# RWKV-5 attention into a top-1 mixture of experts on one Trainium2 core: a new order of turns, sends, logits and weight pieces

## The chip, the cores and the metric

The kernel runs on one core of a Trainium2 chip. The core's engines each run their own instruction stream and meet only at semaphores: TensorE (PE for its matmuls, PEld for its weight loads), VectorE (DVE), ScalarE (ACT), GpSimd (POOL) and SyncE (SP), which here only starts DMA transfers. Matmuls write PSUM, which TensorE, VectorE and ScalarE reach; all else lies in SBUF or in HBM. The metric is the device time of one execution in microseconds (us), as the median of several runs. Lower is better.

## The reference

The attention keeps a 48 x 48 state for each of 4 x 8 (batch, head) pairs over 768 steps; its output is read as 3072 tokens of 384 numbers, and each token goes through one of 8 experts.

```python
for t in range(S):                                   # S = 768
    cur = np.einsum('bhd,bhe->bhde', u[None] * kt, vt)
    y[:, :, t] = np.einsum('bhd,bhde->bhe', rt, state + cur)
    state = w[None, :, :, None] * state + np.einsum('bhd,bhe->bhde', kt, vt)
...
logits = x @ w_gate                                  # x: 3072 x 384
expert_idx = np.argmax(logits, axis=1)
probs = np.exp(logits - logits.max(-1, keepdims=True))
probs /= probs.sum(-1, keepdims=True) + 1e-09
gate_w = probs[np.arange(N), expert_idx]
for e in range(E):                                   # E = 8
    mask = expert_idx == e
    ye = np.maximum(x[mask] @ w1[e], 0.0) @ w2[e]    # 384 -> 1024 -> 384
    out[mask] = gate_w[mask, None] * ye
```

## The kernel before

All of the profiled time is the function `straight`; a second function, `general`, serves inputs that do not fit its assumptions (a decay out of bounds, more than 416 tokens for one expert) and does not run here.

**Attention.** The work is cut into 16 units, unit i = 4 b + hp: batch b, head pair hp. The 768 steps of a unit are 6 chunks of 128. Within a chunk the recurrence is done in closed form: r and k are scaled by powers of the decay (`scale`, L220, VectorE, with the tables `TT`, L114 to 124), the scores of a chunk are one 128 x 128 matmul for each head (`p_scores`, L247), kept only below the diagonal (`mask`, L261, VectorE), with r*u*k on the diagonal. That diagonal comes from `pairs` (L226, the product r*k into `rp`), `p_own` (L235, TensorE sums it with u), `own_t` (L244, VectorE transposes it) and `diag` (L256, twelve pieces on ScalarE that write the identity times the diagonal into `A`; `mask` then puts the scores into the lower part). Between chunks the state is carried: `keys` (L230, GpSimd, k by the decay table `T3`), `p_ds` (L271), `scan` (L279, VectorE). `p_out` (L285, TensorE) multiplies scores and states into `yps`, `out_t` (L304, ScalarE) copies it out. Two units later `p_tr` (L312) turns the result with a selection matrix whose 8 last columns are the gate's weights, so that each token's 96 numbers of this head pair come with 8 partial logits: 104 columns. Chunks 0 to 3 go to the PSUM tile `tr`, chunks 4 and 5 to the same two banks, `X23`, in which `p_scores` puts its chunks 4 and 5 (columns 0 to 255 of a bank; `p_tr` uses 256 to 359). `keep` (L317) copies both into the batch's row buffer `xb` and adds the partial logits up.

**Routing**, once for each batch, from 6 units after its first on: `choose` (L330, argmax and exponentials), `p_rank` (L343) and `slots` (L352) give every token a row in its expert's region of a buffer `rows` in HBM, `gates` (L358) writes the gate into column 96 of every row, `total` (L364) keeps the running counts, and `send` (L369, GpSimd) starts one indirect DMA for each chunk of 128 tokens that scatters their rows. `ids` (L377, GpSimd) writes the token numbers into column 97. It does so ahead of all other writes of its batch, at the end of units 0, 4, 8 and 12. There are two buffers `xb`, so that at units 8 and 12 the buffer must first have been left by the sends of the batch two earlier.

**Experts.** `Pass` (L392) handles up to 416 rows of one expert: `load` (four DMAs), `xT` (VectorE transposes), `L1` (into four PSUM banks, relu on ScalarE), `L2`, and `put` (gate times result, and indirect DMAs by GpSimd that scatter to the output). The first expert is two passes of 256 and 160 rows, so that it can start before the last batch is sent; the last expert's rows from 160 on go through `tokens_out` (L436), 384 wide. Weights are loaded whole (`weights`, L386) into three buffers, two of them there from the start.

**Order.** Each engine works strictly in the order in which the program issues its instructions, and that order is written by hand in the loop over i (L485 to L540). The tile framework adds a wait wherever an instruction touches a tile, or a PSUM bank, that another engine still uses. For unit i the loop issues: `p_own(i)`, `own_t(i)`, `p_scores` of chunks 0 to 3; for a batch that is due, `p_rank` and `slots`; `scale`, `pairs` and `keys` of unit i + 1; `diag(i)`; `p_tr(i-2)`; `p_ds(i)`; `p_scores` of chunks 4 and 5; two masks; `keep(i-2)`; the third mask; `scan(i)`; gates, total and two or three sends; `p_out(i-1)`, `out_t(i-1)`; `choose`, `ids`; the loads of unit i + 3. Loads and weights stand in one queue behind SP, sends behind GpSimd. The tables for all four head pairs are built before the loop: sixteen small VectorE instructions for `TT`, one product `T3c`, four transposes and one copy for `T3`.

Of the kernel before, what the change touches and what calls it, by code (L numbers as in the profile page):

```python
# [29 lines left out]
Q = 2 * D + 2  # L30
CAP = 416
PAD = 320
EARLY = 256
# [7 lines left out]
def straight(tc, rk, vk, w, w1, w2, out, flag):  # L41
# [42 lines left out]
    def load(i):  # L84
        if i >= U:
            return
        b, hp = divmod(i, HP)
        nc.sync.dma_start(rks[i % 3][0:KP], rk[b, hp].rearrange("h p u s -> (h p) u s")[0:KP])
        nc.sync.dma_start(vks[i % 4], vk[b, hp])
# [3 lines left out]
    for i in range(3):  # L93
        load(i)
# [9 lines left out]

# [9 lines left out]
    TT = cp.tile([KP, HP, 2, C], FP32, name="TT")  # L114
    inv = cp.tile([KP, HP], FP32, name="inv")
    nc.vector.reciprocal(inv, pw[:, 6, :])
    nc.vector.tensor_copy(TT[:, :, 0, 0], inv)
    nc.vector.tensor_copy(TT[:, :, 1, C - 1], inv)
    for l in range(7):
        n = 1 << l  # L120
        wn = bc(pw[:, l, :, None], [KP, HP, n])
        nc.vector.tensor_tensor(TT[:, :, 0, n:2 * n], TT[:, :, 0, 0:n], wn, op=ALU.mult)
        nc.vector.tensor_tensor(TT[:, :, 1, C - 2 * n:C - n], TT[:, :, 1, C - n:C], wn, op=ALU.mult)  # L123

    T3c = cp.tile([KP, HP, C], FP32, name="T3c")
    nc.vector.tensor_tensor(T3c, TT[:, :, 1, :], bc(pw[:, 7, :, None], [KP, HP, C]), op=ALU.mult)
    T3 = cp.tile([128, HP, 2 * D], FP32, name="T3")

    def key_decay():
        for hp in range(HP):  # L130
            nc.tensor.transpose(tr[:, hp * 128:hp * 128 + KP], T3c[:, hp, :], ident[0:KP, 0:KP])
        nc.scalar.copy(T3.rearrange("p a (h d) -> p a h d", h=2),
                       tr.rearrange("p (a h d) -> p a h d", a=HP, h=2)[:, :, :, 0:D])
# [13 lines left out]
    def state_decay():  # L147
        nc.gpsimd.memset(dec, 0.0)
        nc.gpsimd.tensor_copy(dec[:, :, :, 1:], bc(pw[:, 7, :, None, None], [KP, HP, D, G - 2]))

# [30 lines left out]
    w1s = [cp.tile([128, DT, F], FP32, name=f"w1s{i}") for i in range(2)]  # L181
    w2s = [cp.tile([128, FT, DM], FP32, name=f"w2s{i}") for i in range(2)]
# [19 lines left out]
    lgs = [ca.tile([128, G, E], FP32, name=f"lg{i}") for i in range(2)]  # L202
    sub, ex, eq = [ca.tile([128, G, E], FP32, name=n) for n in ("sub", "ex", "eq")]
# [10 lines left out]
    def prep(i):  # L214
        if i < U:
            scale(i)
            pairs(i)
            keys(i)

# [6 lines left out]
    def pairs(i):  # L226
        x = rks[i % 3]
        nc.gpsimd.tensor_tensor(rps[i % 2][0:KP], x[0:KP, 0], x[0:KP, 1], op=ALU.mult)  # L228

    def keys(i):  # L230
        hp, v = i % HP, vks[i % 4]
        nc.gpsimd.tensor_tensor(Kds[i % 2], v[:, G:2 * G - 1, :], bc(T3[:, hp, None, :], [128, G - 1, 2 * D]),  # L232
                                op=ALU.mult)
# [74 lines left out]
    W_ = 2 * D + E  # L308
# [8 lines left out]
    def keep(i):  # L317
        b, hp = divmod(i, HP)
        nc.vector.tensor_copy(xbs[b % 2][:, 0:4, hp, 0:2 * D], trv[0][:, :, 0:2 * D])
        nc.scalar.copy(xbs[b % 2][:, 4:G, hp, 0:2 * D], trv[1][:, :, 0:2 * D])  # L320
        for cs, t in ((slice(0, 4), trv[0]), (slice(4, G), trv[1])):
            lg, l = lgs[b % 2][:, cs], t[:, :, 2 * D:]
            if hp == 0:
                nc.vector.tensor_copy(lg, l)
            else:
                nc.vector.tensor_tensor(lg, l, lg, op=ALU.add)
# [3 lines left out]
    def choose(b):  # L330
        lg, oh = lgs[b % 2], ohs[b % 2]
# [8 lines left out]

    rp = tr[:, 4 * W_:4 * W_ + G * E].rearrange("p (c e) -> p c e", e=E)

# [38 lines left out]
    def count(dst):  # L381
        nc.tensor.matmul(tr[:, 480:480 + E], lhsT=ones, rhs=osum, start=True, stop=True, skip_group_check=True)
# [102 lines left out]
    for i in range(U + 1):  # L485
# [16 lines left out]
        if not last:  # L502
            diag(i)
# [612 lines left out]
```

## Time and profile before

| | us |
|---|---|
| median of 14 runs | 432.23 |
| lowest, highest | 427.46, 435.14 |
| the profiled execution | 428.85 |
| its span in the trace | 427.1 |
| PE busy in the span | 391.5 (92%) |
| PEld, DVE, ACT, POOL busy | 263.5, 147.3, 112.3, 189.9 |
| first matmul of the experts (L417) starts | 145.64 |
| mean granted TensorE clock | 0.969 |

The trace records one execution. A line of a view names a source line (L253), an engine and an operation with its tiles, output first. "Busy" is the time in which an engine executes; matmuls are pipelined, and their weight loads (PEld) run beside them. The granted clock is the share of full speed that TensorE was given. The page's rows over time divide the span into 40 slices and give each engine's busy share in tenths. The chain of waits goes back from the last instruction: at each step to what released it. Each group of instructions by line shows the mean duration of one. As context for the steps of the loop, these are the groups of some of its lines (how many instructions, and the mean of one):

| line | engine, what | count | mean ns |
|---|---|---|---|
| L222 | DVE, `scale`, 112 x 1536 | 16 | 2057 |
| L228 | POOL, `pairs`, 112 x 768 | 16 | 2133 |
| L253 | PE, `p_scores`, 128 columns | 384 | 328 |
| L259 | ACT, `diag`, 128 x 128 | 192 | 388 |
| L371 | POOL, one send | 24 | 1249 |
| L417 | PE, `L1` (three widths together) | 432 | 475 |
| L467 | POOL, one `put` transfer | 96 | 983 |

### The profile page before, as it was taken

The page shows a single profiled execution, that of the slowest core. Times are in us where ns is not written, and L with a number is a line of the kernel's source. Part 1 is how long each engine was busy: PE and PEld are TensorE (multiplying, and loading weights), DVE is VectorE, ACT ScalarE, POOL GpSimd, SP SyncE. Part 2 cuts the span into 40 slices and gives each one's busy share as a digit, 9 for nine tenths or more (in the row PEclk, how much of TensorE's full clock was granted, in tenths as well). Part 3 has the DMA queues.
Part 4 walks back from the last instruction along what each step waited for, and adds up shares of the span by engine and source line. Part 5 has one row for each costly group of instructions (what it writes and reads, how often), then busy time and mean ns, then how long its engine had stood idle before and what let it go on. Part 6 is the DMA issues. An engine that isn't in the chain of part 4 may idle for free.

```text
span 427.1 us, 6777 instructions
## 1 busy us (share of the span) xinstructions
PE 391.5 (92%) x2659; PEld 263.5 (62%) x2659; DVE 147.3 (34%) x324; ACT 112.3 (26%) x318; POOL 189.9 (44%) x189
## 2 busy tenths in 40 slices
PE   1799999799769699999999999999999999999993
PEld 0588788588558588858555555555555555455661
DVE  6888887568645221211101201301211211212020
ACT  1567576547534220320200210110120120001100
POOL 4998529539355022250400650560470370276641
PEclk9999999869958999999999999999999999999998
DMA  8956887938902614940900830650560480011101
GB/s 214 274 159 193 241 244 227 317 109 289 374 5 91 210 38 129 344 82 3 345 28 2 254 151 0 188 221 0 135 276 5 80 328 8 11 38 33 32 22 44
DMA packets 26761, 61.36 MB, mean 144 GB/s; under 512 B 17143, under 2 KB 18179, under 8 KB 24672
## 3 DMA queue, kind: packets, MB, share of 16 engines
q1 hardware_dynamic: 21984, 51.29, 38.6%
q0 software_dynamic: 4736, 9.55, 6.4%
q8 instruction: 23, 0.38, 0.4%
q14 instruction: 18, 0.15, 0.1%
HBM read 50.08 MB, written 11.13 MB: 143 GB/s over the span
## 4 chain that ended last, share of the span: by engine, by line
PE 77%; POOL 6%; DMA 5%; DVE 5%; ACT 3%; issue 3%; SPq 0%; POOLq 0%; ACTq 0%; DVEq 0%
PE X L417 32%; PE yps L428 19%; PE dsb L428 10%; DMA rows<-xb,slot 4%; PE X L253 4%; ACT A L259 3%; PE yps L296 3%; PE tr L314 2%; POOL rp L228 2%; POOL rows L371 2%; PE dsb L276 2%; PE dsb L241 2%; PE yps L447 1%; PE dsb L447 1%; PE yps L301 1%
## 5 line engine op out<-in xcount | busy, mean ns | idle before, releaser
L467 POOL DMA_INDIRECT out_dram<-yo,ix x96 | 94.3, 983 | 158.2 <-DVE yo L464 112.2
L417 PE MATMUL X<-xT,w1s 128*128 128x416 f32 (+2 forms) x432 | 136.2, 475 | 3.3 <-DVE xT L409 2.1
L417 PEld LDWEIGHTS X<-xT,w1s 128*128 128x128 f32 x432 | 79.1, 190 | 58.0 <-issue 52.8
L419 ACT ACTIVATE hT<-X 128x416 f32<-128x416 f32 (+2 forms) x72 | 34.5, 479 | 221.7 <-PE X L417 208.5
L428 PE MATMUL yps<-hT,w2s 128*128 128x416 f32 (+2 forms) x288 | 85.8, 451 | 0.7 <-DVE yq L430 0.7
L428 PEld LDWEIGHTS yps<-hT,w2s 128*128 128x128 f32 x288 | 51.4, 190 | 33.4 <-issue 31.2
L259 ACT ACTIVATE A<-ident,own 128x128 f32<-128x128 f32 x192 | 57.9, 388 | 16.1 <-DVE own L245 15.4
L430 DVE STREAM_TRANSPOSE yq<-yps 128x416 f32<-128x416 f32 (+2 forms) x18 | 9.7, 537 | 126.8 <-PE yps L428 126.8
L371 POOL DMA_INDIRECT rows<-xb,slot x24 | 30.0, 1249 | 46.4 <-DVE osum L367 31.8
L428 PE MATMUL dsb<-hT,w2s 128*128 128x416 f32 (+2 forms) x144 | 42.8, 450 | 0.0
L228 POOL TENSOR_TENSOR rp<-rk 112x768 f32<-112x768 f32 x16 | 34.1, 2133 | 9.4 <-DVE TT L123 4.9
L253 PE MATMUL X<-RK 48*128 48x128 f32 x384 | 35.7, 328 | 1.6 <-DVE RK L222 1.6
L428 PEld LDWEIGHTS dsb<-hT,w2s 128*128 128x128 f32 x144 | 25.7, 190 | 15.7 <-issue 15.3
L253 PEld LDWEIGHTS X<-RK 48*128 48x128 f32 x384 | 28.8, 221 | 8.8 <-issue 5.9
L222 DVE TENSOR_TENSOR RK<-rk,TT 112x1536 f32<-112x1536 f32 x16 | 32.8, 2057 | 0.0
L409 DVE STREAM_TRANSPOSE xT<-xs 128x416 f32<-128x416 f32 (+2 forms) x27 | 13.1, 535 | 50.9 <-DMA xs<-rows 50.9
L241 PE MATMUL dsb<-rp,wug 112*2 112x192 f32 x128 | 9.4, 369 | 20.3 <-POOL rp L228 18.1
L296 PE MATMUL yps<-A,vk 128*48 128x128 f32 x384 | 27.0, 296 | 0.0
L296 PEld LDWEIGHTS yps<-A,vk 128*48 128x48 f32 x384 | 22.8, 134 | 2.3 <-issue 0.4
L265 DVE COPY_PREDICATED A<-strict,X 128x512 f32<-128x512 int32 x32 | 22.7, 729 | 4.1 <-ACT A L259 4.1
L232 POOL TENSOR_TENSOR Kd<-vk,T 128x480 f32<-128x480 f32 x16 | 21.7, 1358 | 2.0 <-PE dsb L276 1.3
L306 ACT COPY yT<-yps 112x384 f32<-112x384 f32 x32 | 13.8, 482 | 32.6 <-PE yps L301 32.6
(104 smaller groups left out, 231.2 us busy)
## 6 DMA issues: line engine op xcount, KB each, us to landing
w1s<-in_w_dram SPq DMA_DIRECT2D x8, 1536.0 KB, 8.3
w2s<-in_w_dram SPq DMA_DIRECT2D x8, 1536.0 KB, 11.5
rk<-in_rk_dram SPq DMA_DIRECT2D x16, 672.0 KB, 6.3
vk<-in_vk_dram SPq DMA_DIRECT2D x16, 528.0 KB, 4.3
xs<-rows SPq DMA_DIRECT2D x28, 159.2 KB, 3.9
out_dram<-yo,ix POOLq DMA_INDIRECT x96, 3.8
rows<-zt SPq DMA_DIRECT2D x1, 1176.0 KB, 8.6
xs<-rows SPq DMA_DIRECT2D x4, 98.0 KB, 2.5
```

Of the source, the lines that this page charges most:

```text
L222: nc.vector.tensor_tensor(RKs[i % 3][0:KP].rearrange("p u (c t) -> p u c t", t=C), x[0:KP].rearrange("p u (c t) -> p u c t", t=C), bc(TT[: ...
L228: nc.gpsimd.tensor_tensor(rps[i % 2][0:KP], x[0:KP, 0], x[0:KP, 1], op=ALU.mult)
L232: nc.gpsimd.tensor_tensor(Kds[i % 2], v[:, G:2 * G - 1, :], bc(T3[:, hp, None, :], [128, G - 1, 2 * D]), op=ALU.mult)
L253: nc.tensor.matmul(o, lhsT=r[q, 1, c * C:(c + 1) * C], rhs=r[q, 0, c * C:(c + 1) * C], start=True, stop=True, skip_group_check=True)
L259: nc.scalar.activation(A[:, place(c, h), :], ident, func=ACT.Copy, scale=own[i % 2][:, c, h:h + 1])
L265: nc.vector.copy_predicated(A[:, 4 * k:4 * k + 4, :], bc(m[:, None, :], [128, 4, C]), X01[k])
L296: nc.tensor.matmul(o(c, h), lhsT=v[:, c, h * D:(h + 1) * D], rhs=A[:, place(c, h), :], start=c < 2, stop=c == 0, skip_group_check=True)
L371: s_ = nc.gpsimd.indirect_dma_start(out=rows[:, :], out_offset=bass.IndirectOffsetOnAxis(ap=slot[b % 2][:, c:c + 1], axis=0), in_=xbs[b % ...
L417: nc.tensor.matmul(p[:, 0:self.n], lhsT=w1s[self.e % 3][:, m, f * 128:(f + 1) * 128], rhs=self.t[:, m, 0:self.n], start=m == 0, stop=m == ...
L419: nc.scalar.activation(h[:, f, 0:self.n], p[:, 0:self.n], func=ACT.Relu)
L428: nc.tensor.matmul(p[:, 0:n], lhsT=w2s[self.e % 3][:, f, m * 128:(m + 1) * 128], rhs=self.h[:, f, 0:n], start=f == 0, stop=f == FT - 1, sk ...
L467: s_ = nc.gpsimd.indirect_dma_start(out=out4[:, :], out_offset=bass.IndirectOffsetOnAxis(ap=ix[:, k:k + 1], axis=0), in_=yo[:, k, :], in_o ...
```

## The change

What it does, in the order of the code:

- The loads of r, k and of v, k by chunk are split (`load_rk` at the head of a unit, `load_vk` at its end).
- `p_fill(n)` issues n matmuls of the identity that nobody reads: 14 at the start, 4 in each of units 1 and 2.
- The decay tables are built for one head pair at a time (`decays`, `key_decay`, `p_key_decay`), with both halves of `TT` in one instruction: pair 0 ahead of the loop, pair i + 1 in units 0, 1 and 2. `pairs(0)` and four of the `keys` go to VectorE.
- `turn`: GpSimd copies one element of `own(i)`, so that its work on unit i + 1 starts behind `own_t(i)`.
- A row has 104 columns (`Q`), not 98: the partial logits stay in it, and columns 96 and 97 (gate, number) lie over the first two of them. `keep` is two ScalarE copies of full width, and `choose` sums the four partial logits in one instruction for each batch.
- In the loop, the masks and `p_ds` move ahead of `p_rank`, and `p_tr(i-2)` and `keep(i-2)` ahead of `p_scores` of chunks 4 and 5.
- The results of `p_rank` and `count` lie in the bank `dsb`, no longer in `tr`.
- `ids(b)` comes directly behind `gates(b)` and `total(b)` of its own batch; the sends follow a table, one or two for each of the next units (batch 2: two, then four).
- Weights lie in pieces (`w1` in four, `w2` in three column blocks of 128), in two buffers, each piece refilled as soon as its last use is behind; at the end experts 0 and following are loaded once more without use (`e % E`). `tokens_out` therefore multiplies in 3 x 128 columns.

```diff
-Q = 2 * D + 2
+Q = 2 * D + E
...
-    def load(i):
-        if i >= U:
-            return
-        b, hp = divmod(i, HP)
-        nc.sync.dma_start(rks[i % 3][0:KP], rk[b, hp].rearrange("h p u s -> (h p) u s")[0:KP])
-        nc.sync.dma_start(vks[i % 4], vk[b, hp])
+    def load_rk(i):
+        if i < U:
+            b, hp = divmod(i, HP)
+            nc.sync.dma_start(rks[i % 3][0:KP], rk[b, hp].rearrange("h p u s -> (h p) u s")[0:KP])
+    def load_vk(i):
+        if i < U:
+            b, hp = divmod(i, HP)
+            nc.sync.dma_start(vks[i % 4], vk[b, hp])
...
+    def p_fill(n):
+        for _ in range(n):
+            nc.tensor.matmul(tr[:, 384:512], lhsT=ident, rhs=ident, start=True, stop=True, skip_group_check=True)
...
+    p_fill(14)
...
-    nc.vector.tensor_copy(TT[:, :, 0, 0], inv)
-    nc.vector.tensor_copy(TT[:, :, 1, C - 1], inv)
-    for l in range(7):
-        n = 1 << l
-        wn = bc(pw[:, l, :, None], [KP, HP, n])
-        nc.vector.tensor_tensor(TT[:, :, 0, n:2 * n], TT[:, :, 0, 0:n], wn, op=ALU.mult)
-        nc.vector.tensor_tensor(TT[:, :, 1, C - 2 * n:C - n], TT[:, :, 1, C - n:C], wn, op=ALU.mult)
...
+    def two(h0, nh, first, second, n):
+        a = TTf[:, h0 * 2 * C + first:h0 * 2 * C + first + n]
+        return bass.AP(a.tensor, a.offset, [list(a.ap[0]), [2 * C, nh], [second - first, 2], [1, n]])
+    def decays(h0, nh):
+        nc.vector.tensor_copy(two(h0, nh, 0, 2 * C - 1, 1), bc(inv[:, h0:h0 + nh, None, None], [KP, nh, 2, 1]))
+        for l in range(7):
+            n = 1 << l
+            nc.vector.tensor_tensor(two(h0, nh, n, 2 * C - 2 * n, n), two(h0, nh, 0, 2 * C - n, n),
+                                    bc(pw[:, l, h0:h0 + nh, None, None], [KP, nh, 2, n]), op=ALU.mult)
+    def key_decay(h0, nh):
+        nc.vector.tensor_tensor(T3c[:, h0:h0 + nh, :], TT[:, h0:h0 + nh, 1, :],
+                                bc(pw[:, 7, h0:h0 + nh, None], [KP, nh, C]), op=ALU.mult)
+    def p_key_decay(h0, nh):
+        for hp in range(h0, h0 + nh):
             nc.tensor.transpose(tr[:, hp * 128:hp * 128 + KP], T3c[:, hp, :], ident[0:KP, 0:KP])
-        nc.scalar.copy(T3.rearrange("p a (h d) -> p a h d", h=2),
-                       tr.rearrange("p (a h d) -> p a h d", a=HP, h=2)[:, :, :, 0:D])
+        nc.scalar.copy(T3[:, h0:h0 + nh].rearrange("p a (h d) -> p a h d", h=2),
+                       tr[:, h0 * 128:(h0 + nh) * 128].rearrange("p (a h d) -> p a h d", a=nh, h=2)[:, :, :, 0:D])
...
+    turn = cp.tile([1, 1], FP32, name="turn")
...
-    w1s = [cp.tile([128, DT, F], FP32, name=f"w1s{i}") for i in range(2)]
-    w2s = [cp.tile([128, FT, DM], FP32, name=f"w2s{i}") for i in range(2)]
+    w1s = [[cp.tile([128, DT, FQ], FP32, name=f"w1s{i}{q}") for q in range(4)] for i in range(2)]
+    w2s = [[cp.tile([128, FT, 128], FP32, name=f"w2s{i}{m}") for m in range(DT)] for i in range(2)]
...
+    def pairs(i, eng=None):
         x = rks[i % 3]
-        nc.gpsimd.tensor_tensor(rps[i % 2][0:KP], x[0:KP, 0], x[0:KP, 1], op=ALU.mult)
-    def keys(i):
+        (eng or nc.gpsimd).tensor_tensor(rps[i % 2][0:KP], x[0:KP, 0], x[0:KP, 1], op=ALU.mult)
+    def keys(i, eng=None):
         hp, v = i % HP, vks[i % 4]
-        nc.gpsimd.tensor_tensor(Kds[i % 2], v[:, G:2 * G - 1, :], bc(T3[:, hp, None, :], [128, G - 1, 2 * D]),
-                                op=ALU.mult)
+        (eng or nc.gpsimd).tensor_tensor(Kds[i % 2], v[:, G:2 * G - 1, :], bc(T3[:, hp, None, :], [128, G - 1, 2 * D]),
+                                         op=ALU.mult)
...
     def keep(i):
         b, hp = divmod(i, HP)
-        nc.vector.tensor_copy(xbs[b % 2][:, 0:4, hp, 0:2 * D], trv[0][:, :, 0:2 * D])
-        nc.scalar.copy(xbs[b % 2][:, 4:G, hp, 0:2 * D], trv[1][:, :, 0:2 * D])
-        for cs, t in ((slice(0, 4), trv[0]), (slice(4, G), trv[1])):
-            lg, l = lgs[b % 2][:, cs], t[:, :, 2 * D:]
-            if hp == 0:
-                nc.vector.tensor_copy(lg, l)
-            else:
-                nc.vector.tensor_tensor(lg, l, lg, op=ALU.add)
+        nc.scalar.copy(xbs[b % 2][:, 0:4, hp, :], trv[0])
+        nc.scalar.copy(xbs[b % 2][:, 4:G, hp, :], trv[1])
...
+        nc.vector.tensor_reduce(lg, xbs[b % 2][:, :, :, 2 * D:].rearrange("p c a e -> p c e a"), axis=AX, op=ALU.add)
...
-    rp = tr[:, 4 * W_:4 * W_ + G * E].rearrange("p (c e) -> p c e", e=E)
+    rp = dsb[:, 432:432 + G * E].rearrange("p (c e) -> p c e", e=E)
...
-    def weights(e, which=None):
-        if which in (None, 0):
-            nc.sync.dma_start(w1s[e % 3], w1[e])
-        if which in (None, 1):
-            nc.sync.dma_start(w2s[e % 3], w2[e])
+        nc.tensor.matmul(dsb[:, 480:480 + E], lhsT=ones, rhs=osum, start=True, stop=True, skip_group_check=True)
+        nc.vector.tensor_tensor(dst, dsb[:, 480:480 + E], basef, op=ALU.subtract)
+    def weights1(e):
+        for q in range(4):
+            nc.sync.dma_start(w1s[e % 2][q], w1[e % E, q])
+    def weights2(e, ms=range(DT)):
+        for m in ms:
+            nc.sync.dma_start(w2s[e % 2][m], w2[e % E, m])
...
+                p, y = ybank[t], yt[t].rearrange("p (a m i) -> p m a i", a=HP, m=DT)
+                for m in range(DT):
+                    o = p[:, m * 128:(m + 1) * 128]
+                    for f in range(FT):
+                        nc.tensor.matmul(o, lhsT=self.h[:, f, LAST + t * 128:LAST + (t + 1) * 128],
+                                         rhs=w2s[self.e % 2][m][:, f, :], start=f == 0, stop=f == FT - 1,
+                                         skip_group_check=True)
...
+    sends = {}
+    for b in range(B - 1):
+        for k, cs in enumerate(((0,), (1, 2), (3, 4), (5,)) if b < B - 2 else ((0, 1), (2, 3, 4, 5))):
+            sends[4 * b + 6 + k] = (b, cs)
+    decays(0, 1)
+    scale(0)
+    pairs(0, nc.vector)
+    key_decay(0, 1)
     state_decay()
+    p_scores(0, range(2))
     p_own(0)
     own_t(0)
-    scale(0)
-    key_decay()
+    p_key_decay(0, 1)
     keys(0)
     for i in range(U + 1):
         last = i == U
         b, k = divmod(i - 6, 4)
-        rt = i >= 6
+        rt = i >= 6 and k == 0 and b < B - 1
+        load_rk(i + 3)
         if not last:
             if i > 0:
                 p_own(i)
                 own_t(i)
-            p_scores(i, range(4))
-        if rt and k == 0:
-            p_rank(b)
-            slots(b)
-        prep(i + 1)
+            nc.gpsimd.tensor_copy(turn, own[i % 2][0:1, 0, 0:1])
+            p_scores(i, range(4) if i > 0 else range(2, 4))
+            if 0 < i < 3:
+                p_fill(4)
+        if i + 1 < U:
+            if i + 1 < HP:
+                decays(i + 1, 1)
+            scale(i + 1)
+            if i + 1 < HP:
+                key_decay(i + 1, 1)
+                p_key_decay(i + 1, 1)
+            pairs(i + 1)
+            keys(i + 1, nc.vector if i in (7, 8, 11, 12) else None)
         if i == 0:
             selection()
         if i == 2:
             numbers()
         if not last:
             diag(i)
+            mask(i, 0)
+            mask(i, 1)
+            p_ds(i)
+        if rt:
+            p_rank(b)
+            slots(b)
+        if not last:
+            scan(i)
         if 2 <= i:
             p_tr(i - 2)
-        if not last:
-            p_ds(i)
-            p_scores(i, range(4, G))
-            mask(i, 0)
-            mask(i, 1)
-        if 2 <= i:
             keep(i - 2)
         if not last:
+            p_scores(i, range(4, G))
             mask(i, 2)
-            scan(i)
-        if rt and k < 3:
-            if k == 0:
-                gates(b)
-                total(b)
-            m = 3 if b == B - 2 else 2
-            send(b, range(m * k, min(m * k + m, G)))
+        if rt:
+            gates(b)
+            total(b)
+            ids(b)
+        if i in sends:
+            send(*sends[i])
         if 1 <= i:
             p_out(i - 1)
             out_t(i - 1)
         if i % 4 == 1 and i > 4:
             choose((i - 5) // 4)
-        if i % 4 == 0 and i < U:
-            ids(i // 4)
-        load(i + 3)
-        if i == 4:
+        load_vk(i + 3)
+        if i == 3:
             clear()
-        if i in (9, 11):
-            weights(0, (i - 9) // 2)
+        if i in (12, 13):
+            (weights1, weights2)[i - 12](0)
         if i == 14:
-            weights(1, 0)
+            weights1(1)
+        if i == U - 1:
             count(cnt3)
             nc.vector.tensor_scalar(out=viol[:, 12:13], in0=cnt3[:, 0:1], scalar1=float(EARLY), scalar2=None, op0=ALU.is_lt)
-        if i == U - 1:
+            weights2(1, range(2))
             first.load()
-            weights(1, 1)
+            weights2(1, range(2, DT))
...
     total(B - 1)
+    ids(B - 1)
     send(B - 1, range(G))
...
-    weights(2)
...
+    for k in range(2, n):
+        p, o = passes[k], passes[k - 1]
+        if k < n - 1:
+            p.L1()
+            passes[k + 1].xT()
+            weights1(p.e + 2)
+            o.L2()
+            o.put()
+            if o.e + 2 <= E:
+                weights2(o.e + 2)
+        else:
+            o.L2()
+            p.L1()
+            weights1(p.e + 2)
+            o.put()
         if k + 2 < n:
             passes[k + 2].load()
-        if passes[k].e + 2 < E:
-            weights(passes[k].e + 2)
-    passes[-2].L2()
-    passes[-1].L1()
-    passes[-2].put()
-    passes[-1].L2(n=LAST)
-    passes[-1].put(LAST)
-    passes[-1].tokens_out()
+    p.L2(n=LAST)
+    p.put(LAST)
+    p.tokens_out()
```

## The prediction

> **What bounds the kernel now.** I read four views: the page's rows over time, the stretches, the chain of waits, the timeline. A digit of the page is a fortieth of the 427.1 us span, 10.7 us.
>
> ```profile
> PE   1799999799769699999999999999999999999993
> PEclk9999999869958999999999999999999999999998
> ```
>
> From the 14th slice on TensorE is full: there the mixture of experts runs at TensorE's own pace, and nothing but TensorE's work or a late tile can move it. The losses are in the first 13 slices, in the loop over 16 units. Three stretches of that loop (stretch, length, then busy us of PE, PEld, DVE, ACT, POOL, then granted clock, DMA share, GB/s):
>
> ```profile
> 67.10:73.70 6.60, 6.60 (x114) 5.52 (x116) 5.30 (x9) 4.68 (x15) 6.00 (x5) 1.00 0.75 249
> 73.70:83.30 9.60, 6.59 (x110) 5.46 (x108) 6.20 (x14) 5.68 (x18) 5.03 (x5) 0.99 0.88 277
> 83.30:94.90 11.60, 11.16 (x119) 9.38 (x123) 6.73 (x16) 3.93 (x13) 4.45 (x4) 0.56 0.43 156
> ```
>
> The first is an undisturbed unit. The second has the same work and a 3 us hole; the third does it at a granted clock of 0.56. The chain names both (start, us, what):
>
> ```profile
> 32.98 0.44 PE dsb L241 x8
> 33.42 1.09 PE X L253 x16
> 34.51 1.07 PE tr L314 x8
> 35.58 0.45 PE X L314 x4
> 36.03 0.58 PE dsb L276 x20
> 36.61 0.65 PE X L253 x8
> 37.26 1.45 PE yps L296 x24
> 38.71 0.83 PE yps L301 x20
> ...
> 75.07 6.12 DMA rows<-xb,slot
> 81.50 1.80 POOL rp L228
> 83.34 0.86 PE dsb L241 x8
> ```
>
> The upper eight are a unit: 0.44 + 1.09 + 1.07 + 0.45 + 0.58 + 0.65 + 1.45 + 0.83 = 6.56 us, all TensorE, end to end. The lower three are the hole: GpSimd's ids (L378) waits for sent rows to leave, its product L228 stands behind, TensorE's L241 behind that. The chain's L241 pieces give the unit starts: 9.15, 18.21, 26.43, 32.98, 39.5, 46.8, 53.3, 60.6, 67.1, 73.7, 83.3, 94.9, 101.4, 107.9, 120.5, 132.4. Units 3 to 14 so take 99.4 us, against 12 x 6.56 = 78.7: 20.7 us are loss, of which the holes before units 10 and 14 and the slow clock behind them are 19.4 (3.1 + 5.0 + 6.0 + 5.3).
>
> **The change, part by part.** *Ids, sends, turns.* `ids(b)` now stands behind its own batch's gates, so it waits for no row of that batch, and the sends are spread. The 20.7 us go, if nothing takes their place.
>
> *What takes their place.* keep(i-2) now comes ahead of p_scores(i, 4..5), and both use bank X23. In the program as built the first of these matmuls waits for ScalarE's copy out of X23 in the same unit; in the kernel before it didn't. That copy is the last of 14 on ScalarE:
>
> ```profile
> 68.17 3.62 ACT L259 ACTIVATE A<-ident,own 128x128 f32<-128x128 f32 x12
> 71.69 0.30 ACT L320 COPY xb<-X 128x192 f32<-128x192 f32 x1
> ...
> L419 ACT ACTIVATE hT<-X 128x416 f32<-128x416 f32 x56 | 29.0, 517 | 196.7 <-PE X L417 196.7
> ```
>
> The unit began at 67.12. The twelve diag pieces start 1.05 into it, and the next ScalarE instruction can start at 4.57. There the change puts first the copy from tr, which was VectorE's and is now 416 wide: 0.52 by the L419 row of that width, 0.42 until the next can follow (L306's two 0.48 copies start 0.38 apart). Then the X23 copy, 208 wide against 192: 0.31. It ends at 4.57 + 0.42 + 0.31 = 5.30; with 0.05 for the signal (L306 to L314 at 139.5) the scores start at 5.35. Until then TensorE has p_own, four scores, p_ds and p_tr, ready at 3.63. Queued behind: scores 0.65, p_out 1.45 + 0.83, and with them the next unit's p_own. The unit is 8.28, say 8.3. Bounds: 8.1 if the copies overlap more, 8.5 if signals cost more. Twelve units: 12 x 8.3 = 99.6, as good as the 99.4 of before. The whole gain is given back here.
>
> Will the hole of 1.7 us cost the clock? The rows: TensorE stood 2.10 us before 145.64, and six 256-wide matmuls then took 1.56; the later 24 took 5.45, or 1.36 for six. It kept the clock. After the 3.05 us hole at 83.3 it had lost it. I take none lost. [...]
>
> *Start-up.* Tables come one pair at a time, and ScalarE's copy of T3 for unit i+1 stands ahead of diag(i) for i = 0, 1, 2. Unit 0: rk lands by 6.77 (L228 starts then, and it needs only rk); the pair's eight small table steps are done before, at 0.19 each (L113). scale 1.72, the product now on VectorE 0.86 (half of L222's width): p_own near 9.4, own_t done by 10.4. Then VectorE runs eight more steps (1.6), scale(1) 1.72, T3c 0.25; TensorE transposes, ScalarE copies (0.3 each); only then diag(0) starts, 4.2 us behind own_t instead of 0.1. [...]
>
> ```profile
> 10.34 4.77 DVE L222 TENSOR_TENSOR RK<-rk,TT 112x1536 f32<-112x1536 f32 x2
> 11.51 1.99 POOL L232 TENSOR_TENSOR Kd<-vk,T 128x480 f32<-128x480 f32 x1 [0.68 <-ACT T L132]
> 13.46 3.33 POOL L228 TENSOR_TENSOR rp<-rk 112x768 f32<-112x768 f32 x1
> ```
>
> Two products of VectorE need 4.77 where 3.44 would do: the engines take turns. [...] From diag's start, eight pieces 2.4, mask 0.73, scan 0.64 free the next p_own. Unit 0: 10.4 + 4.2 + 3.8 = 18.4, up to 21.4. Unit 1: 0.95 to own_t, then 4.2 and 3.8, so 9.0, up to 10.9. Unit 2 has keep too: 0.95 + 4.2 + 3.52 + 0.73 + 0.65 + 2.28 = 12.3, up to 15.9 with the port's 1.8 and a slow clock (p_out was 3.1 at 23.2). Unit 3 starts at 39.7 to 48.2, against 32.98. The rows above show sharing as the rule, so I take 46.5: +13.5. The 14 fill matmuls (28 instructions at 0.25, the slow L314) run from 1.5 to 8.5, when scale ends: nothing, one us if they overrun. [...]
>
> *Sends and keep.* keep of units 10 and 14 must wait for the batch's last row, sent one unit earlier. It is sent about 6 us into unit 9 or 13; landings were 2.6 to 8.8 us, and ScalarE asks 12.9 us after that unit's start. All weights up to w2s(1) are now issued at the end of unit 12, 5.5 MB, so unit 14 may wait: 0 to 3, say +0.5. A send beside a VectorE product took 2.05 us instead of 0.98 (68.63), in GpSimd's slack. [...]
>
> *Last rows.* Batch 2 sends two rows in unit 14 behind total (8.1) and four in unit 15: 1.3 each, ending 7.4 into unit 15 against 6.8 before. The first expert's rows and L417 follow: +0.6 (bounds -1.2, where p_out is last, and +2).
>
> *Experts.* tokens_out makes 48 matmuls of 128 columns out of 16 of 384. Before: 5.43 + 5.17 = 10.6. The nearest rows, L314 with 104 columns and fresh weights, take 0.225 to 0.268: 10.8 to 12.9. I take 0.25: 12.0, +1.4, at the very end.
>
> *At nothing.* Weight pieces: a buffer is refilled about 50 us (three passes of 16.76) before its use and lands in 8 to 12; with a late load it would cost its lateness. About 40 more SP issues at 0.45 over 270 us. keys on VectorE in four units (0.69 by L126): VectorE has 5.3 busy of 8.3. The logit sum and the turn (0.2 each) fall into the same slack. Without it each adds itself. The three repeated weight loads at the end come while TensorE has 17 us and more to go.
>
> **Sum.** Start-up +13.5, loop +0.2, send +0.5, last rows +0.6, tokens +1.4: +16.2. The profiled execution took 428.85 us (span 427.1 and 1.75 around it), 3.4 under the median 432.23. So 445.0 like for like, 448.4 as a median.
>
> **Rivals.** *The wait is hidden* and a unit stays 6.56: -21, so 427 (420 with start-up at its low bound): faster. For it: ScalarE is busy only 4.68 of 6.6. Against: it can't start diag before own_t, and the order is fixed. *The clock is lost in the holes* (the trace has none of 1.7 in every unit): TensorE's own work doubles, a unit is some 11.3 (2.2 + 2.9 of p_own to p_tr and so on, as at 83.3), about every other one: 6 x 3 = +18, 466. Against: 2.10 us held. *Turns do nothing*: scale stays 3.4 in places; in an 8.3 us unit that hides, +0. *Half hidden*, units of 7.0 or so: 432.
>
> **How the numbers follow.** Forecast 0.76, lost clock 0.09, hidden 0.11, half hidden 0.04. Forecast's own range: start-up -6.8 to +1.7, unit 8.1 to 8.5 (2.4 either way), send -0.5 to +2.5, last rows -1.8 to +1.4, tokens -1.2 to +0.9; the medians before lay 3 us about 432. Taken together about 436 to 460; to 464 for part of the lost clock. Outside are hidden, half hidden and the upper clock case, under 0.2. A measurement of this kernel tells about 0.5% from none: faster 0.11, same 0.04, slower 0.85.
>
> **What would show it.** Right: the chain passes ScalarE's A and xb before each late X; L241 comes every 8.3 us; unit 3 starts near 46; no GpSimd wait on sent rows; tokens_out at 12. Wrong: L241 every 6.6 us, or unit 3 before 38. A granted clock near 0.6 in the loop means the lost clock.

## The result and the profile after

The changed kernel takes 467.13 us (median of 10 runs, 463.95 to 472.92) against 432.01 (47 runs of the kernel before); the ratio is 1.0835, with a 95% interval of 1.0799 to 1.0872. (Ratios here compare only those executions of the two kernels that ran in the faster of two states, so they differ a little from the quotient of the medians.) It was forecast slower, at 448.4: the direction was right, the size half. The profiled execution has a span of 463.6 us against 427.1: 36.5 us more.

The two rows of the page over time, each digit a fortieth of the span (11.6 us):

```profile
PE   7386888987788879999999999999999999999993
PEclk8557777588888898999999999999999999999998
```

Before, most slices of the loop showed a 9 in TensorE's row; now one of the first 15 does, and the row of the granted clock has no 9 in its first 14. From the 17th slice on both rows are full but for the end, as they were before. Times of the two profiled executions by stage, with unit starts read from the timeline:

| stage | before | after | difference |
|---|---|---|---|
| start to unit 3 | 32.91 | 50.45 | +17.5 |
| unit 3 to unit 15 | 99.41 | 116.97 | +17.6 |
| unit 15 to the first expert's L1 | 13.32 | 14.53 | +1.2 |
| experts | 281.5 | 281.7 | +0.2 |

The chain of waits in one unit of the loop (start, us, what), from its first L258 to the next:

```profile
101.57 0.48 PE dsb L258 x8
102.14 0.39 DVE own L262
102.62 3.62 ACT A L276 x12
106.24 0.39 ACT xb L336
106.62 0.24 ACT xb L337
106.90 0.71 PE X L270 x8
107.62 2.31 PE yps L313 x24
109.93 1.45 PE yps L318 x20
```

This is the wait that was forecast: TensorE's p_own, VectorE's own_t, ScalarE's twelve diag pieces, then its copies out of `tr` and out of X23, and only then p_scores of chunks 4 and 5. But p_out (L313, L318) behind it takes 2.31 + 1.45 us, not 1.45 + 0.83. Three units as stretches (stretch, length, busy us of PE, PEld, DVE, ACT, POOL, granted clock, DMA share, GB/s):

```profile
101.57:111.38 9.81, 8.10 (x112) 6.57 (x116) 5.14 (x7) 5.09 (x16) 5.89 (x4) 0.83 0.52 172
111.38:120.88 9.50, 7.78 (x112) 6.21 (x116) 6.07 (x12) 5.09 (x16) 5.49 (x4) 0.86 0.50 154
120.88:129.53 8.65, 7.15 (x121) 5.71 (x123) 5.80 (x13) 5.23 (x17) 4.65 (x5) 0.95 0.40 136
```

The third has almost the forecast length of 8.3; there the granted clock is 0.95. The others lose 1.2 to 1.5 us more, with the clock at 0.83 to 0.86: TensorE works on them 8 us instead of 6.6. Of the twelve units 3 to 14, nine take 9.5 to 9.9 us; unit 6 takes 12.05, at a clock of 0.53, and units 10 and 14 take 8.65 and 8.44. The wait itself costs what was said, and something else comes on top.

GpSimd's row waits are gone, as forecast: the view of waits had `ids` (L378) waiting 11.3 us for sent rows; in the changed kernel no wait of GpSimd on sent rows is left in it.

### The profile page after: what moved, and what is told of

Read it like the earlier page. It is cut to its first block, busy times and chain, and to the rows that moved or that the text cites. A ratio compares the mean times of both kernels' runs of the same rounds, so it can differ in the third digit from the quotient of the medians.

```text
span 463.6 us, 7143 instructions
## 1 busy us (share of the span) xinstructions
PE 416.0 (90%) x2767; PEld 286.8 (62%) x2767; DVE 147.6 (32%) x304; ACT 119.0 (26%) x337; POOL 189.5 (41%) x200
## 4 chain that ended last, share of the span: by engine, by line
PE 78%; ACT 12%; DVE 3%; issue 2%; POOL 0%; POOLq 0%; DVEq 0%; ACTq 0%
PE X L431 29%; PE yps L442 18%; ACT A L276 10%; PE dsb L442 9%; PE yps L313 8%; PE yps L318 4%; PE X L270 4%; PE dsb L258 2%; DVE TT L143 1%; PE yps L463 1%; ACT xb L336 1%; PE dsb L463 1%; DVE own L262 1%; PE tr L331 1%; ACT xb L337 1%
## 5 line engine op out<-in xcount | busy, mean ns | idle before, releaser
L518 POOL COPY turn<-own 1x1 f32<-1x1 f32 x16 | 21.7, 1358 | 53.0 <-DVE own L262 45.6
L313 PE MATMUL yps<-A,vk 128*48 128x128 f32 x384 | 36.7, 365 | 0.0
L383 POOL DMA_INDIRECT rows<-xb,slot x24 | 24.0, 1002 | 21.8 <-DVE osum L379 12.0
L313 PEld LDWEIGHTS yps<-A,vk 128*48 128x48 f32 x384 | 30.5, 166 | 2.6 <-issue 0.9
L239 DVE TENSOR_TENSOR RK<-rk,TT 112x1536 f32<-112x1536 f32 x16 | 27.6, 1727 | 0.4 <-DMA rk<-in_rk_dram 0.3
L245 POOL TENSOR_TENSOR rp<-rk 112x768 f32<-112x768 f32 x15 | 27.1, 1805 | 0.0
L249 POOL TENSOR_TENSOR Kd<-vk,T 128x480 f32<-128x480 f32 x12 | 14.3, 1196 | 18.0 <-ACT T L153 18.0
```

What stands on the lines that cost most here:

```text
L239: nc.vector.tensor_tensor(RKs[i % 3][0:KP].rearrange("p u (c t) -> p u c t", t=C), x[0:KP].rearrange("p u (c t) -> p u c t", t=C), bc(TT[: ...
L245: (eng or nc.gpsimd).tensor_tensor(rps[i % 2][0:KP], x[0:KP, 0], x[0:KP, 1], op=ALU.mult)
L313: nc.tensor.matmul(o(c, h), lhsT=v[:, c, h * D:(h + 1) * D], rhs=A[:, place(c, h), :], start=c < 2, stop=c == 0, skip_group_check=True)
L383: s_ = nc.gpsimd.indirect_dma_start(out=rows[:, :], out_offset=bass.IndirectOffsetOnAxis(ap=slot[b % 2][:, c:c + 1], axis=0), in_=xbs[b % ...
L518: nc.gpsimd.tensor_copy(turn, own[i % 2][0:1, 0, 0:1])
```

## The experiments

There are fourteen runs. Each set of runs has its own executions of the kernel before beside it, and a ratio is to those. The first set is `fill4`, `scores_first`, `tables_once` and `keep_dve`.

### Does the hole cost the clock?

`fill4` puts four matmuls that nobody reads into the hole, and leaves every wait.

```diff
+    def p_warm(n):
+        for _ in range(n):
+            nc.tensor.matmul(yps[:, 0, 384:512], lhsT=ident, rhs=ident, start=True, stop=True, skip_group_check=True)
...
             p_tr(i - 2)
+            p_warm(4)
             keep(i - 2)
```

> The changed kernel with four more matmuls of the identity, which nobody reads, behind p_tr(i-2) in every unit; every wait stays. Theory (the wait on X23 leaves a hole of 1.7 us, and the hole itself costs the clock): the matmuls take about 1.1 us, the hole is 0.6, the clock stays at 1.00, p_out takes 1.45 + 0.83 in every unit and a unit 8.3 us instead of 9.75: 12 x 1.45 = 17 us less, about 449. Rival (p_out is slow for another reason, such as the copies of the other engines beside it): p_out stays at 2.0 to 2.7 and the time at 466.

The stretches of three of its units (columns as above):

```profile
83.51:91.83 8.32, 7.53 (x118) 6.38 (x116) 5.14 (x7) 5.09 (x16) 6.87 (x5) 1.00 0.66 213
91.83:100.17 8.34, 7.54 (x119) 6.39 (x118) 5.16 (x7) 5.09 (x16) 5.90 (x4) 1.00 0.65 200
100.17:108.50 8.33, 7.53 (x119) 6.38 (x118) 5.91 (x12) 5.09 (x16) 5.51 (x4) 1.00 0.67 187
```

With the hole at 0.8 us instead of 1.7 the clock is 1.00, and units 3 to 14 take 100.3 us instead of 117.0. More work made the loop 16.6 us faster; so the slow p_out came from the hole. The rival falls.

The time does not show it: 467.65 us, ratio 1.062 (1.056 to 1.069). In this set the kernel before took 440.5 us, 8 more than elsewhere. In the trace of `fill4` ScalarE stops several times for 3 to 6 us, and the trace names no instruction of this core that releases it. One such stop, of 4.1 us, falls in unit 15; in the last expert TensorE waits for ScalarE, 2.1 and 8.2 us. So the first expert comes 19.8 us behind unit 15 instead of 14.5, and the experts take 295.3 us instead of 281.7. The other three kernels of the set have the same stops (experts of 292.9 to 296.0). They belong to these executions and not to the kernels: `keep_dve` run again in another set has none, and its experts take 281.2 us instead of 296.0. What stops the engines stays open. The stages that the stops do not touch can still be compared.

### What does undoing the order give?

`scores_first` moves one line back: p_scores of chunks 4 and 5 ahead of p_tr and keep.

```diff
+        if not last:
+            p_scores(i, range(4, G))
         if 2 <= i:
             p_tr(i - 2)
             keep(i - 2)
         if not last:
-            p_scores(i, range(4, G))
             mask(i, 2)
```

> The changed kernel with p_scores of chunks 4 and 5 put back ahead of p_tr(i-2) and keep(i-2). Theory: no wait on X23, units of 6.6 us, 12 x (9.75 - 6.6) = 38 us less, about 428; the start-up stays (unit 3 starts near 48). Rival (another wait of the new order takes its place: diag and copies on ScalarE, the turn of GpSimd, the scan): units of 8 or more, 445 and up.

Units take 6.55 us where nothing else holds them (6.55 to 7.48, all at clock 1.00), and the loop from unit 3 to 15 takes 84.1 us instead of 117.0. Unit 3 still starts at 48.97. The first expert starts at 151.1 instead of 182.0, 31 us earlier; the same stops in the experts take 12 us of it back. The ratio is 1.019 (1.013 to 1.025); that of the changed kernel was 1.0835, beside a faster kernel before. One unit in the chain, TensorE from end to end again:

```profile
75.52 0.44 PE dsb L258 x8
75.95 1.09 PE X L270 x16
77.04 0.58 PE dsb L293 x20
77.63 0.65 PE X L270 x8
78.27 1.07 PE tr L331 x8
```

`before_order` makes the same kind of loss in the kernel before, by moving only that line behind keep.

```diff
             p_ds(i)
-            p_scores(i, range(4, G))
             mask(i, 0)
             mask(i, 1)
         if 2 <= i:
             keep(i - 2)
         if not last:
+            p_scores(i, range(4, G))
             mask(i, 2)
```

> The kernel before with one edit: p_tr(i-2) stays where it is, and p_scores of chunks 4 and 5 come behind the masks and keep(i-2), as in the change. Theory: they wait for the reads of X23 in keep, in every unit; a hole near 1.5 us, units of 8.1 us, in part with the clock lost (9.5), and the loop from unit 3 to 15 takes 105 to 115 us instead of 99; ratio 1.015 to 1.04. Rival (the wait comes only with the other edits): units of 6.6 us, ratio 1.00.

452.38 us, ratio 1.046 (1.038 to 1.053). The loop takes 121.9 us instead of 99.4: four units of 8.05 to 8.85 at a clock of 0.96 to 1.00, eight of 9.6 to 12.7 at 0.73 to 0.84. There the late scores wait for VectorE's sum of the logits (L326), the last reader of X23 in that kernel, with holes of 1.4 to 1.5 us in seven units and of 2.3 to 3.7 in five. The order alone, in a kernel that has nothing else of the change, costs 22.5 us of the loop, somewhat more than expected.

### What does the start-up owe to the tables?

`tables_once` builds all four pairs' tables ahead of the loop again, with the changed kernel's own functions.

```diff
-    decays(0, 1)
+    decays(0, HP)
...
-    key_decay(0, 1)
+    key_decay(0, HP)
...
-    p_key_decay(0, 1)
+    p_key_decay(0, HP)
...
-            if i + 1 < HP:
-                decays(i + 1, 1)
...
-            if i + 1 < HP:
-                key_decay(i + 1, 1)
-                p_key_decay(i + 1, 1)
```

> The changed kernel with the tables of all four pairs built ahead of the loop, as before the change; all else as changed. Theory (the start-up is lost to table steps and their copies that stand ahead of diag in units 0 to 2, and to GpSimd's product between the steps): unit 3 starts near 36 us instead of 50.5, about 452. Rival (the start-up is lost to the order of the masks and to the turn, not the tables): unit 3 still at 45 or later, 461 and up.

Unit 3 starts at 33.68 instead of 50.45: the tables explain 16.8 of the 17.5 us. The loop stays at 115.9. As in the rest of that set, ScalarE stops for 4.1 us in the last unit and the experts take 292.9 us, so the ratio falls only to 1.056 (1.046 to 1.067). Where the time goes can be read in the changed kernel's unit 1. Three lines of VectorE, then one of GpSimd:

```profile
22.74 0.38 DVE L262 STREAM_TRANSPOSE own<-dsb 128x192 f32<-128x192 f32 x1 [0.40 <-PE dsb L258]
23.21 3.24 DVE L143 TENSOR_TENSOR TT<-TT,pw 112x2 f32<-112x2 f32 x7
26.48 1.76 DVE L239 TENSOR_TENSOR RK<-rk,TT 112x1536 f32<-112x1536 f32 x1
...
23.39 1.81 POOL L245 TENSOR_TENSOR rp<-rk 112x768 f32<-112x768 f32 x1
```

Seven tiny steps take 3.24 us. The chain puts 1.83 of it on the first of them (`23.41 1.83 DVE TT L143`), the time of GpSimd's product beside it. The turn that is to keep the engines apart lets GpSimd start right behind own_t, and there the small steps stand. ScalarE's diag waits for all of it: it starts at 29.12 in unit 1, 6.0 us behind own_t's end.

### Both together, and the parts of the gain

`both` joins the two mends. `after_again` and `before_again` ran beside it.

> The changed kernel with p_scores of chunks 4 and 5 ahead of p_tr and keep, and with all tables built ahead of the loop. Theory (the two causes add up): unit 3 starts near 33, unit 15 near 117, the first expert near 133 against 145.6 of the kernel before; a ratio of about 0.975 to the kernel before. Rival (DMA at the end of the loop, or stalls, take it back): the first expert at 143 or later, ratio 1.0.

> The changed kernel itself once more, beside the others of this call, since the chip of the first four runs took 440.5 us for the kernel before. If the four differences of the first call were those of the chip, its ratio to the kernel before is 1.08 here too and units are 9.75 us with half of their p_out at half clock.

> The kernel before itself, for a trace from the same chip as the others of this call: where it stands above 428.85, the trace shows in which stage the chip is slower. Theory: the units are those of the first trace and the excess lies in the experts, where engines stop without a releaser in the trace. Rival: all stages are slower by the same share.

The changed kernel again: 466.18 us, ratio 1.082 (1.075 to 1.089), ten of the twelve units at 9.5 to 9.9 again. `both`: 416.52 us, ratio 0.966 (0.959 to 0.973), the fastest version of the study with `both_sends`, and faster than either kernel. Its rows over time:

```profile
PE   6899999999984999999999999999999999999992
PEclk9599999999997799999999999999999999999998
```

Unit 3 starts at 33.43 and the loop takes 80.2 us, 1.5 above twelve undisturbed units. The two causes add up to the whole loss in both stages, and uncover the gain of the loop that the change was forecast to bring and give back: 19.3 us against the kernel before. Not all of it reaches the end. The 13th slice of TensorE's row and the 13th and 14th of the clock show where; this is TensorE's line there, the first expert's first six matmuls:

```profile
130.98 2.93 PE L431 MATMUL X<-xT,w1s 128*128 128x256 f32 x6 [5.22 <-DVE xT L423]
```

TensorE stands 5.2 us until the first expert's rows have come; in the kernel before it stood 2.1 there, and the six matmuls took 1.56 us instead of 2.93. The granted clock is 0.68 over the 15 us from 130.98. The first expert starts 17.4 us behind unit 15 instead of 13.3, and the experts take 286.1 us instead of 281.5, so that 8.7 of the 19.3 us are lost again, most of them to the same pair of costs, a hole and the slow clock behind it.

`before_again` took 434.16 us; its loop sums to 98.4 us although single units differ by up to 5 us from the first trace, and 4.1 of the 5.3 us by which its span is longer lie in the experts. The rival of equal shares falls. The theory's stops do not appear either: here too TensorE stands longer ahead of the first expert (3.9 us) and starts it with 2.93 us for the six matmuls.

What in the change makes the gain? `before_ids` moves `ids` in the kernel before:

```diff
                 gates(b)
                 total(b)
+                ids(b)
...
-        if i % 4 == 0 and i < U:
-            ids(i // 4)
...
     total(B - 1)
+    ids(B - 1)
```

> The kernel before with one edit: ids(b) behind gates(b) and total(b) of its own batch, as in the change. Theory (GpSimd's wait for sent rows in ids makes the two holes and the slow clock behind them): no unit above 7.4 us, the first expert near 127 instead of 145.6, ratio 0.957. Rival (keep must wait for the same rows two units later): one hole in each of the two places remains, ratio 0.98 or more.

432.23 us, ratio 1.000 (0.994 to 1.005): nothing. The wait for rows is gone, and a new one stands in its place. VectorE's line of one small step, then GpSimd's lines beside it:

```profile
81.92 4.47 DVE L333 TENSOR_TENSOR sub<-lg,mx 128x48 f32<-128x48 f32 x1
...
80.42 1.84 POOL L228 TENSOR_TENSOR rp<-rk 112x768 f32<-112x768 f32 x1
82.20 1.22 POOL L232 TENSOR_TENSOR Kd<-vk,T 128x480 f32<-128x480 f32 x1
83.36 1.81 POOL L228 TENSOR_TENSOR rp<-rk 112x768 f32<-112x768 f32 x1
85.12 1.19 POOL L232 TENSOR_TENSOR Kd<-vk,T 128x480 f32<-128x480 f32 x1
```

A 128x48 step that took 0.21 us in each of its four places in the kernel before takes 4.47 us. It begins beside one product of GpSimd and ends at 86.39, when the third one behind that ends (86.31). GpSimd, no longer held by `ids`, ran a unit ahead, into VectorE's routing steps; that unit took 14.66 us. The rival had the time (0.98 or more) but another cause: the chain of that unit passes through this step and no wait for rows. `before_ids_turn` adds the turn to it:

```diff
+    turn = cp.tile([1, 1], FP32, name="turn")
...
                 own_t(i)
+            nc.gpsimd.tensor_copy(turn, own[i % 2][0:1, 0, 0:1])
             p_scores(i, range(4))
```

> The kernel before with ids behind the gates of its own batch, and with the turn (GpSimd copies one element of own(i) ahead of pairs and keys of unit i + 1). Theory (moving ids alone gave nothing, since GpSimd's products then met small steps of VectorE: 4.47 us for L333): with the turn no VectorE step of 128x48 takes over 2 us, units are 6.6 to 7.3, the first expert starts near 130, ratio 0.965. Rival (the turn does nothing for it): as without, ratio 1.00.

428.13 us, ratio 0.990 (0.986 to 0.993): L333's counterpart is down to 1.65 us at most and the loop to 92.8 us, a third of the expected gain. `both_noturn` asks the same from the other end, by deleting that line from `both`.

> The version with both mends (scores first, tables at once) without the turn. Theory: GpSimd's products fall on small VectorE steps, a few units of 8 us and more, the loop from unit 3 to 15 takes 85 to 95 us instead of 80, ratio 0.98 to 1.0. Rival (with ids moved and sends spread the turn is not needed): ratio 0.966 as with it.

423.18 us, ratio 0.980 (0.974 to 0.987); the loop takes 87.5 us instead of 80.2, with one unit of 12.36 in which the same step takes 2.97 us. The turn is worth some 7 us of the loop there. `both_sends` packs the sends closer.

```diff
-        for k, cs in enumerate(((0,), (1, 2), (3, 4), (5,)) if b < B - 2 else ((0, 1), (2, 3, 4, 5))):
+        for k, cs in enumerate(((0, 1), (2, 3), (4, 5)) if b < B - 2 else (range(G),)):
```

> The version with both mends, and the sends of batches 0 and 1 as two in each of three units, those of batch 2 all in unit 14. Theory: keep of units 10 and 14 no longer waits for a row sent one unit before (1.4 us in unit 14), the last row leaves 2 to 3 us earlier, the first expert starts 3 to 4 us sooner (near 127); 412, ratio 0.957. Rival (the sends' descriptors then hold VectorE's products in the same units): no gain, ratio 0.966 or more.

418.76 us, ratio 0.968 (0.961 to 0.975): no gain. The sends of batch 2, the last ones in the loop, start at 115.92, against 116.17 for the first two of them in `both`; they wait for gates and total, which stand in VectorE's queue behind mask(14, 2) and so behind ScalarE's copy out of X23. Earlier places in the table of sends do not move that.

### Which hole costs the clock?

`keep_dve` puts the copy out of `tr` back on VectorE, so that ScalarE reaches X23 0.4 us earlier. Its first run spread from 458.2 to 469.9 us, which allows no comparison, so it was repeated, beside `fill1`, which is `fill4` with one matmul.

```diff
-        nc.scalar.copy(xbs[b % 2][:, 0:4, hp, :], trv[0])
+        nc.vector.tensor_copy(xbs[b % 2][:, 0:4, hp, :], trv[0])
```

> The changed kernel with the copy out of tr back on VectorE; the copy out of X23 stays on ScalarE behind diag, and the order stays. Theory: ScalarE reaches the X23 copy 0.4 us earlier, the hole is 1.3 us, under half of a stretch of 3.4 us; the clock stays, units are 7.9 us, about 444. Rival (any hole above 1 us costs the clock): units of 9.3, about 461.

> The changed kernel with the copy out of tr on VectorE, once more, for an undisturbed run. Theory (half of a stretch): holes of 1.3 us keep the clock, units of 7.9 us, the loop from unit 3 to 15 takes 95 us, ratio 1.03. Rival (size alone does not decide): units of 7.9 and 9.5 side by side, 100 us and more, ratio 1.04 to 1.06.

> The changed kernel with one more matmul of the identity behind p_tr(i-2) in every unit. Theory (the clock is lost where a stretch of 3.4 us is idle by about half, 1.7 us, and kept at 1.5): the hole is 1.45 us, the clock stays, units of 8.3 us, as with four matmuls. Rival (holes above 1.2 us lose it, depending on what else lies in the stretch): units of 8.3 and of 9.8 us side by side, the loop from unit 3 to 15 between 105 and 115 us.

`keep_dve` the second time: 450.12 us, ratio 1.042 (1.037 to 1.047); holes of mostly 1.31 us, seven units of 7.93 to 7.99 at clock 0.99 or 1.00 and five of 9.5 to 9.6 at 0.82. `fill1`: 459.69 us, ratio 1.065 (1.058 to 1.072); holes of mostly 1.46 us, five units of 8.33 to 8.48 and seven of 9.7 to 9.9. So the theory that half of a stretch decides falls, and the rival holds: size alone does not decide.

In the trace of the changed kernel the granted clock steps between 1.00 and 0.50 at 24 times from 9.04 to 176.30 us, each a whole number of 3.41 us behind the one before. Two pairs of neighbouring stretches of that length in `fill1`:

```profile
71.42:74.84 3.42, 1.96 (x28) 1.65 (x29) 1.98 (x4) 1.83 (x7) 2.12 (x2) 1.00 0.33 94
74.84:78.25 3.41, 3.41 (x76) 2.63 (x72) 2.80 (x9) 1.90 (x7) 0.86 (x1) 1.00 0.51 172
88.49:91.90 3.41, 1.95 (x18) 1.76 (x19) 2.72 (x5) 3.04 (x11) 3.25 (x3) 1.00 0.71 270
91.90:95.32 3.42, 3.42 (x40) 2.84 (x40) 0.73 (x1) 0.00 (x0) 1.47 (x2) 0.53 0.35 125
```

Both first stretches are idle for 1.46 us; behind the one the clock stays at 1.00, behind the other it reads 0.53 over the whole stretch. (The borders given here can be off by 0.2 us: the 0.53 in the last line, instead of 0.50, says that the clock changed that much later.) In the one that kept it TensorE came back at 73.31, 1.5 us before its end, and 28 matmul instructions stand in it; in the other at 91.58, 0.3 before its end, with 18. A long time between the return and the border is not the rule, though. In `fill1` another stretch lost the clock with TensorE back at 111.35 for 112.38, in the changed kernel one with TensorE back at 75.64 for 77.30, and in `keep_dve_again` one kept it though its hole ended with it (98.66 for 98.60).

What these runs do show is a size. In the stretches of 3.41 us read from the loops of the kernel before, the changed kernel, `fill4`, `fill1`, `tables_once` and both runs of `keep_dve`, none at full clock with less than 1.14 us of idle time was followed by half clock, all with more than 1.73 us were, and in between it went either way. Idle time is not the whole of it: in unit 6 of the changed kernel the clock stayed at 0.50 from 77.31 to 90.96, though TensorE was never idle in three of those four stretches. What decides there, the amount or kind of work in the stretch perhaps, is open.

## Why the prediction was off

**The wait on X23: right, in place and size.** The late scores were to start 5.35 us into the unit; they start at 106.90 - 101.57 = 5.33 by the chain (5.40 by the timeline, where the unit starts at 101.50). A unit was to take 8.3 us at full clock; in `fill4`, where the clock stays, ten of twelve take 8.32 to 8.34, and the loop 100.3 against a forecast of 99.6.

**The clock: the step that failed.** "The rows: TensorE stood 2.10 us before 145.64 ... It kept the clock. ... I take none lost." One hole was read as a rule. Cut into stretches of 3.41 us, that hole lies across a border, so no stretch holds the whole of it. The stretches of the kernel before:

```profile
141.51:144.92 3.41, 2.03 (x42) 1.63 (x38) 0.17 (x2) 0.97 (x3) 0.00 (x0) 1.00 0.83 169
144.92:148.34 3.42, 2.70 (x18) 2.54 (x18) 1.32 (x4) 0.38 (x1) 0.00 (x0) 1.00 0.95 392
```

It is 1.38 us of idle time in the first and 0.71 in the second; if the border is put where the clock's own changes in that trace (83.20, 93.44, 117.33, 130.99) put it, 0.3 us earlier, it is 1.09 and 1.01, both below the least that cost the clock in those loops (1.14, in `keep_dve_again`). The holes of the changed kernel mostly lie whole in a stretch:

```profile
104.61:108.02 3.41, 1.70 (x22) 1.41 (x22) 2.22 (x5) 2.24 (x8) 2.96 (x3) 1.00 0.17 50
108.02:111.43 3.41, 3.41 (x44) 2.66 (x44) 0.45 (x1) 0.00 (x1) 0.97 (x1) 0.50 0.49 151
```

1.71 us idle, and the next 3.41 us run at a granted clock of 0.50; so it went with all nine stretches of its loop that were idle for as long. In the loop this costs 117.0 - 100.3 = 16.6 us, most of the 20.3 by which the forecast of the span missed (36.5 measured, 16.2 said). The case was among the rivals, at 466, but as a unit of 11.3 us every second time; in fact nearly every unit loses about 1.5. That its time fits the 467.13 is in part luck: the start-up was 4 us longer than the sum had it, and smaller terms fell short. It got 0.09 because one row was taken against it. In these runs stretches idle for 1.71 us, and some for 1.3, were enough.

**Start-up: right mechanism, too small.** +13.5 was said, +17.5 measured, above the upper bound of 48.2 for unit 3. diag was to start 4.2 us behind own_t in units 1 and 2; it started 6.0 behind, since GpSimd's whole product (1.81) fell among the small steps each time, where part of it had been taken. In unit 0, with `keys` there too, it started 7.0 behind. And in unit 1 the sum followed the wrong engine: it let diag, mask and scan free the next p_own, and left out p_out of unit 0. TensorE's p_ds, late scores and p_out stand behind the transpose of the tables there and run without a gap from 28.88 to 34.20, 1.3 us past the scan's end. The slow clock, at 0.55 and 0.68 in units 1 and 2, lengthens them. The upper ends of the sum for units 0 to 2 (21.4, 10.9, 15.9) count GpSimd's products in full inside the small steps ("the port's 1.8"); no run shows that as a rule, only these cases: the seven steps of a pair's table took 2.09 us ahead of the loop with no product beside them, 4.14 in unit 0 with two, 3.24 and 3.22 in units 1 and 2 with one.

**Ids, sends, turns: right for the whole, not for a part.** The 20.7 us were put down to the place of `ids` and the spread sends. With all of the change's parts and no wait on X23 the loop is 80.2 us, 19.3 below before. But `ids` moved alone gives 0 in the time, and with the turn 6.6 us of the loop. Which other parts of the change (the spread sends, the logits kept in the row, the masks and p_ds moved ahead) give the remaining 12.6 us was not tested.

**The small terms.** keep's wait for sent rows (+0.5 was taken) is not seen in the slow loop of the changed kernel; in faster loops it is there, with 0.2 us in `fill4`, 0.5 in `scores_first` and 1.0 in `both`. The send at 68.63 took 1.93 us; the 2.05 beside which the prediction puts that time stand at 102.81. Unit 15 to the first expert: +0.6 forecast, +1.2 measured. tokens_out: 12.0 forecast, 5.62 + 5.38 = 11.0 measured, against 10.6 before; the rows of 104 columns were the wrong neighbour for a chain of 48 matmuls. The edits taken at nothing (weight pieces, two buffers, repeated loads) cost nothing: the experts take 281.7 us against 281.5.

## What to carry to other kernels

Before an instruction is moved ahead on one engine, look which bank or tile it shares with what now stands behind it: a copy that was last in its queue became the condition of the next matmuls. When a new hole opens on TensorE, price it twice, once as idle time (1.7 us in a unit here) and once as half clock in the stretch behind it (16.6 us of the loop), and do not take a single hole that did no harm for a rule; filling it with matmuls that nobody reads tells the two apart in one run (in `fill4` the clock was 1.00). A wait that is taken away may be what kept two engines apart: after `ids` was freed, GpSimd ran into VectorE's small steps (4.47 us for one of 0.21) and the gain was nil, ratio 1.000, until it was given a turn, ratio 0.990. And a loop that ends sooner meets the next wait sooner: in `both` 8.7 of 19.3 us were lost again in front of and in the first expert.

## What the hardware showed that was not expected

TensorE's granted clock fell to 0.50 for 3.41 us, in unit 6 of the changed kernel for 13.65, behind holes of 1.3 to 1.7 us, and equal holes cost it or not (five of twelve units in `keep_dve_again`, with holes of mostly 1.31 us, and seven of twelve in `fill1`, with mostly 1.46); what decides between them is open. In `before_ids` a VectorE step of 128x48 took 4.47 us instead of 0.21 while GpSimd ran product after product: it began beside one of them and ended with the third behind that (86.39 and 86.31). And in one set of runs ScalarE stopped for 3 to 6 us at a time, and TensorE behind it, with no instruction of the core to release it; the same kernel run again had none of it, and what stops them stays open.
